# Products of a constant tile on TensorE, ahead of an attention and expert kernel's first maxima

## The chip, the cores and the metric

The kernel runs on one core of a Trainium2 chip. The time is the device time of one execution in microseconds, and a kernel's time is the median of its runs. The engines are TensorE (PE, with its loads of weights as PEld), VectorE (DVE), ScalarE (ACT), GpSimd (POOL) and SyncE (SP, which issues most of the transfers). Each has a queue of its own that it works in order.

## The reference

Attention for 4 batches of 8 heads, 576 tokens, 64 columns; its result, 2304 tokens of 512 columns, goes through a layer of 8 experts of which each token uses one.

```python
q_rot, k_rot = (rotate(q), rotate(k))
scores = scale * np.matmul(q_rot, k_rot.transpose(0, 1, 3, 2))
scores = scores - np.max(scores, axis=-1, keepdims=True)
attn = np.exp(scores)
attn = attn / (np.sum(attn, axis=-1, keepdims=True) + 1e-09)
attn_out = np.matmul(attn, v)
...
expert_idx = np.argmax(logits, axis=1)          # logits of x and the experts' embeddings
h = np.maximum(x[mask] @ w1[e], 0.0)
out[mask] = gate_w[mask, None] * (h @ w2[e])
```

## The kernel before

The attention works on 16 pairs of heads. A pair has nine steps: four tiles of 128 tokens for each of its two heads, and step 4, which holds the last 64 tokens of both. Work is put on a list with a due time in steps (`at(time, function, ...)`), pair `i` starting at time `9*i`; the list is sorted and emitted, and each engine works its part of it in that order.

For a pair, these functions matter:

- `rope` rotates q and k by products with cosines and sines (VectorE for pair 0 and for k of pair 1, GpSimd otherwise), casts the result to 16 bits on ScalarE (`qhi`, `khi`, line 133) and takes the rest (`qlo`, `klo`, line 138). `place` copies these by DMA to the operands of the scores (`QAB`, `KA`, `KB`).
- `maxmm` (line 171) multiplies q by k for one step: two products of 288 columns into a tile `mx` of two PSUM banks, columns 0 to 287 of each bank. `maxred` (line 175) takes the maximum of each row on VectorE. For pairs 0 to 2 the operands are `qhi` and `khi` themselves, with 64 rows, so that no copy is waited for. The maxima are only a shift against overflow.
- `maxend` turns a pair's nine maxima on TensorE (`mt`, line 182), casts them to a row on ScalarE and sends it by DMA into row 64 of `QB`.
- `smm` makes the scores of a step: four products of 288 columns (lines 196 and 199) into a tile `st`. `sexp` (line 209) takes the exponential on ScalarE, `ssub` (line 218) splits off the low half on VectorE.
- `ve` (line 112) multiplies v by the experts' embeddings, ten small 32-bit products. `pv` (lines 234 to 239) multiplies the exponentials by v, step by step, seven and a half steps behind the scores.

`mx` and `st` come from one pool `sps` of three tiles, tag `s`: a product into a new tile waits until the tile that stood in that place three tiles earlier was read.

The maxima of pair 0 are due from -21 to -17, those of pair 1 from -5 to 3, a step apart, so that the last four of pair 1 lie between the scores of pair 0; those of pair 2 from 4.5 on. The prologue (`first`, at -60) starts the loads. Behind the attention come the experts' products.

Of the kernel before, what the change touches and what calls it, by code (L numbers as in the profile page):

```python
# [6 lines left out]
F32 = mybir.dt.float32  # L7
F16 = mybir.dt.float16
# [30 lines left out]
def attention(tc, ctx0, ctx, ctx2, ins, xs, R, at, bank, cfg):  # L39
    nc = tc.nc  # L40
# [3 lines left out]
    const = ctx.enter_context(tc.tile_pool(name="aconst", bufs=1))  # L44
# [3 lines left out]
    sps = ctx.enter_context(tc.tile_pool(name="asps", bufs=3, space=PSUM))  # L48

    cost = rp.tile([128, S], F32, name="cost", bufs=1)  # L50
    sint = rp.tile([128, S], F32, name="sint", bufs=1)
    shiftt = const.tile([128, 1], F32, name="shiftt")
    nc.vector.memset(shiftt, SHIFT)
    NB = cfg.get("nb", 4)
# [85 lines left out]
    def place(i, nm, part):  # L140

        n, t = i % NB, st[i][nm + part]
        for h in range(2):
# [9 lines left out]
            else:  # L153
                nc.sync.dma_start(out=KB[n][0:64, c], in_=t[r])

    def maxmm(i, s):
        n = i % NB
        if s == 0:
            st[i]["m9"] = tp.tile([128, 9], F32, tag="m9", name=f"m9_{i}")
        ps = sps.tile([128, 2, 512], F32, tag="s", name=f"mx_{i}_{s}")  # L160
        st["mx", i, s] = ps
        hs = [(0, 64, 0), (64, 64, 1)] if s == 4 else [(0, 128, 0 if s < 4 else 1)]
        for r0, m, h in hs:
            for c in range(2):
                q, k = slice(s * 128 + r0, s * 128 + r0 + m), slice(h * S + c * 288, h * S + c * 288 + 288)
                lt, rt = QA[n][:, q], KA[n][:, k]
                if i < cfg.get("mdir", 1):

                    r = slice(64 * h, 64 * h + 64)
                    lt, rt = st[i]["qhi"][r, q.start - h * S:q.stop - h * S], st[i]["khi"][r, c * 288:c * 288 + 288]  # L170
                nc.tensor.matmul(ps[r0:r0 + m, c, :288], lhsT=lt, rhs=rt, start=True, stop=True)  # L171
# [86 lines left out]
    RL = cfg.get("rlead", 13)  # L258
    PVL = cfg.get("pvlead", 7)
    at(-60, first)  # L260
    for n in range(NB):
        at(-60 + .1 * n, nc.gpsimd.memset, KB[n][64:65, :], 1.0)
    start = cfg["start"]
# [5 lines left out]
    for i in range(NPAIR):  # L269
# [37 lines left out]
        for s in range(9):  # L307
            ev(f"S{s}", g0 + s, smm, i, s)
            ev(f"E{s}", g0 + s + .1, sexp, i, s)
            ev(f"U{s}", g0 + s + cfg.get("sst", 1.05), ssub, i, s)  # L310
            mev(f"M{s}", m0 + md * s + cfg.get("mmt", .2), maxmm, i, s)
            mev(f"C{s}", m0 + md * s + cfg.get("mct", .25), maxred, i, s)
            ev(f"P{s}", g0 + PVL + s + cfg.get("pvt", .3), pv, i, s)
            if s in (4, 8):
                ev(f"X{s // 5}", g0 + PVL + s + cfg.get("pe0", 1.04), pvend, i, s // 5, 0)
                ev(f"Y{s // 5}", g0 + PVL + s + cfg.get("pe1", 1.06), pvend, i, s // 5, 1)
# [403 lines left out]
class Schedule:  # L720
# [3 lines left out]
    def at(self, g, f, *a):  # L724
        self.T.append((g, len(self.T), f, a))
# [13 lines left out]
def build(tc, ins, out, cfg=None):  # L739
    cfg = {**TIMES, **(cfg or {})}  # L740
    nc = tc.nc
    with ExitStack() as ctx:
# [14 lines left out]
        mctx, actx2, actx, actx0 = [ctx.enter_context(ExitStack()) for _ in range(4)]  # L757
        if True:
            PVL = attention(tc, actx0, actx, actx2, ins, xs, R, sc.at, bank, cfg)
            for k in range(6):  # L760
                sc.at(cfg.get("setup", (-59.5, -25, -13, -12, -20, -8))[k], R.setup, k)
# [194 lines left out]
```

## Time and profile before

| | |
|---|---|
| median of 3 runs | 595.16 us (593.59 to 597.38) |
| the profiled execution | 591.15 us, of which the span from the first to the last instruction is 589.4 us |
| TensorE busy | 522.8 us, 89% of the span |
| VectorE busy | 522.4 us, 89% |
| ScalarE, GpSimd busy | 346.0 us (59%), 258.5 us (44%) |

Times in the rows count from the span's start. A row of the timeline has the start, the duration (of all instructions merged in it), engine, source line, operation, output and inputs, and how many; in brackets the idle time ahead of it and what ended it. The durations of products on TensorE are modelled and overlap; the distance from one start to the next tells how fast they run. The granted clock of TensorE is given as a share of its full speed.

### The profile page before, as it was taken

The numbers are of one execution on the slowest core, as the hardware profiler recorded it, in microseconds if no ns is written. First come the engines' busy times: TensorE is split into PE (matmuls) and PEld (weight loads), VectorE is DVE, ScalarE is ACT, GpSimd is POOL, SyncE is SP. The second block draws the span as 40 slices with busy tenths as digits, with TensorE's granted clock in tenths as the row PEclk, the third lists the DMA queues.
The fourth block names the chain that finished last, engine by engine and source line by source line (L and its number), as shares of the span: only waits on it lengthen the run. The fifth ranks groups of instructions, "written<-read, shape, count | busy, mean of one in ns | idle before, by whom it ended". The sixth has DMA issues, their size and how long they took to land. (4 is left out here: it accounts for less than half of the span.)

```text
span 589.4 us, 16094 instructions
## 1 busy us (share of the span) xinstructions
PE 522.8 (89%) x6222; PEld 403.3 (68%) x6222; DVE 522.4 (89%) x810; ACT 346.0 (59%) x578; POOL 258.5 (44%) x162
## 2 busy tenths in 40 slices
PE   1599898898898889788897989999999999999993
PEld 0336687776687777677686977767767767767761
DVE  5988889999999998999896665699999999999981
ACT  2143435464643546246356562588989989989962
POOL 5669847477657576621004231312422422423211
PEclk9999989899998989799898989999999999999998
DMA  8586566468565574423318410268986114431100
GB/s 279 149 246 193 140 172 167 137 172 213 146 179 152 173 202 133 131 73 88 106 47 288 127 29 20 91 206 298 317 302 208 39 57 157 127 137 38 56 20 31
DMA packets 42914, 86.13 MB, mean 146 GB/s; under 512 B 8390, under 2 KB 25670, under 8 KB 42832
## 3 DMA queue, kind: packets, MB, share of 16 engines
q1 hardware_dynamic: 39312, 74.46, 42.5%
q0 software_dynamic: 3520, 10.58, 5.6%
q8 instruction: 51, 0.84, 0.6%
q14 instruction: 31, 0.25, 0.1%
HBM read 115.84 MB, written 10.56 MB: 214 GB/s over the span
## 5 line engine op out<-in xcount | busy, mean ns | idle before, releaser
L652 DVE SCALAR_TENSOR_TENSOR w<-raw,w 128x1024 f16<-128x1024 f32 x148 | 177.0, 1236 | 9.4 <-ACT w L651 9.1
L209 ACT ACTIVATE p<-st 128x576 f32<-128x576 f32 x144 | 93.4, 649 | 136.2 <-PE st L199 134.7
L651 ACT ACTIVATE w<-raw 128x1024 f16<-128x1024 f32 x148 | 148.3, 1055 | 0.0
L688 PEld LDWEIGHTS <-w 128*128 128x128 f16 x2112 | 121.3, 99 | 4.7
L218 DVE TENSOR_TENSOR p<-p 128x576 f16<-128x576 f32 x112 | 124.4, 1115 | 0.0
L688 PE MATMUL h<-xTm,w 128*128 128x128 f16 x2112 | 123.6, 220 | 0.0
L709 PE MATMUL yp<-w,hT 128*128 128x512 f16 x528 | 120.8, 379 | 0.0
L175 DVE TENSOR_REDUCE m<-mx 128x1 f32<-128x576 f32 x144 | 105.1, 747 | 14.1 <-PE mx L171 13.7
L714 POOL DMA_INDIRECT out<-y,sidx x22 | 32.8, 1489 | 159.7 <-ACT y L713 159.7
L239 PE MATMUL pv<-V,p 128*128 128x73 f16 (+1 forms) x640 | 86.1, 202 | 1.7 <-DVE p L218 1.7
L709 PEld LDWEIGHTS <-hT 128*128 128x128 f16 x528 | 50.7, 98 | 53.0 <-issue 0.2
L237 PE MATMUL pv<-V,p 128*128 128x73 f16 (+1 forms) x640 | 86.4, 204 | 0.0
L238 PE MATMUL pv<-V,p 128*128 128x72 f16 (+1 forms) x640 | 86.0, 205 | 0.0
L237 PEld LDWEIGHTS <-p 128*128 128x128 bf16 (+1 forms) x640 | 74.1, 116 | 0.0
L196 PE MATMUL st<-QAB,KA 128*128 128x288 f16 (+1 forms) x320 | 65.1, 309 | 5.9 <-DVE m L175 5.2
L239 PEld LDWEIGHTS <-p 128*128 128x128 f16 (+1 forms) x640 | 67.5, 107 | 2.3 <-DVE p L218 2.3
L238 PEld LDWEIGHTS <-p 128*128 128x128 bf16 (+1 forms) x640 | 67.0, 106 | 0.0
L199 PE MATMUL st<-QAB,KB 65*128 65x288 f16 (+1 forms) x320 | 65.2, 308 | 0.0
L234 PE MATMUL pv<-V,p 128*128 128x73 f32 (+1 forms) x320 | 61.6, 277 | 0.0
L171 PE MATMUL mx<-KA,QAB 128*128 128x288 f16 (+1 forms) x260 | 51.0, 298 | 8.7 <-DVE m L175 5.7
L234 PEld LDWEIGHTS pv<-V,p 128*128 128x128 f32 (+1 forms) x320 | 50.0, 195 | 9.7 <-issue 5.6
L138 POOL TENSOR_TENSOR qlo<-q,qhi 128x576 f16<-128x576 f32 x14 | 20.5, 1465 | 64.4 <-ACT qhi L133 64.4
(157 smaller groups left out, 692.7 us busy)
## 6 DMA issues: line engine op xcount, KB each, us to landing
raw<-w SPq DMA_DIRECT2D x152, 512.0 KB
q<-qk SPq DMA_DIRECT2D x16, 576.0 KB
k<-qk SPq DMA_DIRECT2D x16, 576.0 KB
vt<-vt SPq DMA_DIRECT2D x16, 320.0 KB
v<-v SPq DMA_DIRECT2D x16, 320.0 KB
QAB<-qhi SPq DMA_DIRECT2D x32, 144.0 KB
KA<-khi SPq DMA_DIRECT2D x64, 72.0 KB
xs<-x SPq DMA_DIRECT2D x8, 512.0 KB
```

The costliest lines, as they stand in the source:

```text
L175: nc.vector.tensor_reduce(out=st[i]["m9"][:, s:s + 1], in_=st.pop(("mx", i, s))[:, :, :288], op=ALU.max, axis=AX.XY)
L199: nc.tensor.matmul(ps[r0:r0 + m, c, :288], lhsT=KB[n][0:65, col], rhs=QB[n][0:65, h * S + c * 288:h * S + c * 288 + 288], start=False, sto ...
L209: nc.scalar.activation(out=p.rearrange("p (c x) -> p c x", c=2), in_=st.pop(("s", i, s))[:, :, :288], func=AF.Exp, scale=0.125)
L218: nc.vector.tensor_tensor(out=lo, in0=p, in1=hi, op=ALU.subtract)
L234: nc.tensor.matmul(o[:, 0:73], lhsT=P[ksl][0][:, qc:qc + m], rhs=V32[i % NV][:, h, kk], start=(kk == 0), stop=False, skip_group_check=True)
L237: nc.tensor.matmul(o[:, 0:73], lhsT=ph, rhs=vv[:, 0:73], start=(kk == 0), stop=False, skip_group_check=True)
L238: nc.tensor.matmul(o[:, 1:73], lhsT=ph, rhs=vv[:, 73:145], start=False, stop=False, skip_group_check=True)
L239: nc.tensor.matmul(o[:, 0:73], lhsT=pl, rhs=vv[:, 0:73], start=False, stop=(kk == 4), skip_group_check=True)
L651: nc.scalar.activation(out=d[:, 0], in_=raw[c], func=AF.Copy, scale=SW)
L652: nc.vector.scalar_tensor_tensor(out=d[:, 1], in0=raw[c], scalar=SW, in1=d[:, 0], op0=ALU.mult, op1=ALU.subtract)
L688: nc.tensor.matmul(ps[:, f], lhsT=wd[:, wi, jj * 512 + f * 128:jj * 512 + f * 128 + 128], rhs=xt[:, xi, 2 * jp + jj], start=(jp == 0 and k ...
L709: nc.tensor.matmul(ps, lhsT=ht[:, hi, 2 * c + ii], rhs=wd[:, wi, ii * 512:(ii + 1) * 512], start=(c == 0 and k == 0), stop=(c == 3 and k = ...
```

## The change

A tile `wz` of 128 x 512 ones, 16 bits, is written by VectorE as its first instruction. In the prologue TensorE makes 30 products of `wz` by itself, 512 columns wide, into a tile `warm` of the pool `sps`. In pairs 0 and 1, ahead of the two products of each step but step 4, it makes two products of 224 columns into columns 288 to 511 of that step's own tile `mx`, which nobody reads.

```diff
+    wz = const.tile([128, 512], F16, name="wz")
+    nc.vector.memset(wz, 1.0)
...
+    def warm(n):
+        ps = sps.tile([128, 2, 512], F32, tag="s", name="warm")
+        for _ in range(n):
+            nc.tensor.matmul(ps[:, 0], lhsT=wz[:, 0:128], rhs=wz, start=True, stop=True)
+
     def maxmm(i, s):
...
         st["mx", i, s] = ps
+        if i < 2 and s != 4:
+            for c in range(2):
+                nc.tensor.matmul(ps[:, c, 288:512], lhsT=wz[:, 0:128], rhs=wz[:, 0:224], start=True, stop=True)
         hs = [(0, 64, 0), (64, 64, 1)] if s == 4 else [(0, 128, 0 if s < 4 else 1)]
...
     at(-60, first)
+    at(-58.95, warm, 30)
```

TensorE's queue at the end of pair 0's maxima, before. `mx_8` is the last step's tile, `khi`, `qhi` the rotated operands, `ve` and `mt` as above, and the last `mx_0` is pair 1's:

```order
L171 MATMUL mx_8_263<-khi_200,qhi_181 128x288 [waits DVE_49]
L171 LDWEIGHTS qhi_181
L171 MATMUL mx_8_263<-khi_200,qhi_181 128x288
L112 MATMUL ve_267<-enB,vt_176 128x2x8 [waits DMAHW1_49]
L112 MATMUL ve_267<-enB,vt_176 128x2x8 x4
L182 MATMUL mt_286<-ident,m_0_216 9x128 [waits DVE_49]
L171 LDWEIGHTS qhi_273 [waits PE_49,Activation_49]
L171 MATMUL mx_0_306<-khi_280,qhi_273 128x288 [waits Activation_49]
```

The same place now (lines of the changed file):

```order
L172 LDWEIGHTS wz
L172 MATMUL mx_8_310<-wz 128x224 [waits DVE_49]
L172 MATMUL mx_8_310<-wz 128x224
L182 LDWEIGHTS qhi_214
L182 MATMUL mx_8_310<-khi_233,qhi_214 128x288
L115 MATMUL ve_316<-enB,vt_209 128x2x8 [waits DMAHW1_49]
L115 MATMUL ve_316<-enB,vt_209 128x2x8 x4
L193 MATMUL mt_335<-ident,m_0_249 9x128 [waits DVE_49]
L172 MATMUL mx_0_355<-wz 128x224 [waits PE_49]
L172 MATMUL mx_0_355<-wz 128x224
L182 LDWEIGHTS qhi_322 [waits Activation_49]
L182 MATMUL mx_0_355<-khi_329,qhi_322 128x288 [waits Activation_49]
```

The wait for VectorE, which frees the tile, now stands at the first product of `wz`; the wait for ScalarE's `khi` stays at the real product, so the products of `wz` for pair 1's step 0 stand ahead of it.

TensorE's queue between the first score tile `st_0` and the second, before:

```order
L199 LDWEIGHTS KB_131
L199 MATMUL st_0_340<-QAB_129,KB_131 128x288
L171 LDWEIGHTS qhi_273
L171 MATMUL mx_5_347<-khi_280,qhi_273 128x288 [waits DVE_49]
L171 MATMUL mx_5_347<-khi_280,qhi_273 128x288
L196 LDWEIGHTS KA_130
L196 MATMUL st_1_352<-QAB_129,KA_130 128x288 [waits DVE_49]
```

And now:

```order
L210 LDWEIGHTS KB_133
L210 MATMUL st_0_397<-QAB_131,KB_133 128x288
L172 LDWEIGHTS wz
L172 MATMUL mx_5_404<-wz 128x224 [waits DVE_49]
L172 MATMUL mx_5_404<-wz 128x224
L182 LDWEIGHTS qhi_322
L182 MATMUL mx_5_404<-khi_329,qhi_322 128x288
L207 LDWEIGHTS KA_132
L207 MATMUL st_1_411<-QAB_131,KA_132 128x288 [waits DVE_49]
```

Two products and two loads of weights are new between the score tiles; nothing else has changed places.

## Rows read from the trace of the kernel before

**Rows 1.** The page, busy time (share of the span) and instructions of each engine.

```profile
PE 522.8 (89%) x6222; PEld 403.3 (68%) x6222; DVE 522.4 (89%) x810; ACT 346.0 (59%) x578; POOL 258.5 (44%) x162
```

**Rows 2.** Busy time by stage: length, then PE, PEld, DVE, ACT, POOL, clock, DMA, GB/s.

```profile
13.00:30.00 17.00, 10.39 (x43) 5.87 (x42) 15.38 (x24) 2.46 (x7) 12.15 (x9) 1.00 0.59 154
30.00:46.00 16.00, 14.22 (x57) 5.23 (x56) 13.71 (x15) 7.37 (x13) 11.46 (x8) 1.00 0.85 235
46.00:62.00 16.00, 15.81 (x115) 10.92 (x115) 12.06 (x14) 4.89 (x11) 12.11 (x8) 1.00 0.62 173
62.00:76.00 14.00, 11.87 (x156) 9.60 (x154) 13.86 (x22) 5.90 (x11) 11.59 (x7) 0.99 0.64 174
76.00:79.00 3.00, 3.00 (x29) 2.54 (x28) 3.00 (x6) 1.28 (x4) 0.00 (x0) 0.50 0.51 136
```

**Rows 3.** TensorE's timeline, a maxima's step and the next.

```profile
32.00 0.66 PE L171 MATMUL mx<-khi,qhi 64*128 64x288 f16 x2
...
33.67 0.66 PE L171 MATMUL mx<-khi,qhi 64*128 64x288 f16 x2
```

**Rows 4.** TensorE's timeline, two score steps with value products, and 62 us.

```profile
53.08 0.68 PE L196 MATMUL st<-QAB,KA 128*128 128x288 f16 x2
...
56.00 0.68 PE L196 MATMUL st<-QAB,KA 128*128 128x288 f16 x2
...
62.07 0.24 PE L237 MATMUL pv<-V,p 128*64 128x73 f16 x1
```

**Rows 5.** TensorE's timeline, score steps and `ve` after 62 us.

```profile
65.42 0.41 PE L196 MATMUL st<-QAB,KA 128*128 128x288 f16 x2
...
66.15 0.34 PE L234 MATMUL pv<-V,p 128*128 128x73 f32 x2
...
71.19 0.41 PE L196 MATMUL st<-QAB,KA 128*128 128x288 f16 x2
...
73.28 1.29 PE L112 MATMUL ve<-enB,vt 128*128 128x16 f32 x10 [0.99 <-DVE xe L255]
```

**Rows 6.** TensorE's timeline, from pair 0's last maxima to the first scores.

```profile
23.40 1.30 PE L171 MATMUL mx<-khi,qhi 64*128 64x288 f16 x4 [0.46 <-DVE m L175]
24.63 2.31 PE L112 MATMUL ve<-enB,vt 128*128 128x16 f32 x10
...
27.90 3.07 PE L171 MATMUL mx<-khi,qhi 64*128 64x288 f16 x12 [0.74 <-ACT khi L133]
30.95 0.64 PE L196 MATMUL st<-QAB,KA 128*128 128x288 f16 x2
```

**Rows 7.** VectorE's waits, 26 to 62 us: total us, times, longest.

```profile
DVE m L175 <- PE mx L171: 6.2, 6, 2.2
DVE V L118 <- ACT V L117: 1.3, 1, 1.3
```

**Rows 8.** ScalarE's timeline, behind `ve`.

```profile
26.98 0.27 ACT L116 ACTIVATE V<-ve 128x80 f16<-128x80 f32 x1 [10.17 <-PE ve L112]
...
27.18 0.67 ACT L133 CAST khi<-k 128x576 f16<-128x576 f32 x1
```

**Rows 9.** The first product on TensorE, the first maximum on VectorE.

```profile
13.17 1.60 PE L171 MATMUL mx<-khi,qhi 64*128 64x288 f16 x6 [13.17 <-ACT khi L133]
...
16.98 0.74 DVE L175 TENSOR_REDUCE m<-mx 128x1 f32<-128x576 f32 x1
```

**Rows 10.** VectorE's timeline, its first wait.

```profile
5.45 0.76 DVE L126 TENSOR_TENSOR q<-q,cost 128x576 f32<-128x576 f32 x1 [3.64 <-DMA q<-qk]
```

**Rows 11.** VectorE's timeline, pair 1's last four maxima.

```profile
32.70 0.76 DVE L175 TENSOR_REDUCE m<-mx 128x1 f32<-128x576 f32 x1 [0.47 <-PE mx L171]
34.36 0.76 DVE L175 TENSOR_REDUCE m<-mx 128x1 f32<-128x576 f32 x1 [0.91 <-PE mx L171]
36.03 0.76 DVE L175 TENSOR_REDUCE m<-mx 128x1 f32<-128x576 f32 x1 [0.91 <-PE mx L171]
...
39.75 0.74 DVE L175 TENSOR_REDUCE m<-mx 128x1 f32<-128x576 f32 x1
```

## Prediction, made before the result was known

> **What bounds the kernel now.** I read the page's busy times first. TensorE and VectorE are both busy for 89% of the span [rows 1], which does not say what the first 80 us are worth, and the change lies there alone. The table of stages [rows 2] is the next view. In 30 to 46 us TensorE is busy 14.22 of 16 us and VectorE 13.71; in 46 to 62 us TensorE is busy 15.81 and VectorE only 12.06; in 62 to 76 us it is the other way round (11.87 against 13.86 of 14). So TensorE limits up to 62 us and VectorE limits after that.
>
> The reason is TensorE's clock. The granted clock in [rows 2] reads 1.00 up to 76 us and 0.50 in 76 to 79 us, but before 62 us I trust the spacing of the products instead: the first change that it shows is the fall at 76 us, so the 1.00 ahead of it may be no record at all. Between 32.00 and 33.67 us six products of 288 columns start one behind the other, 0.278 us each [rows 3]; between 65.42 and 66.15 us six products of the same width take 0.73 us, 0.122 us each [rows 5]. That is the lower of the two levels (1.2 GHz) before, the upper (2.4 GHz) after; the change is at 62.07 us, where products of 73 columns shorten from 0.26 us [rows 4]. The price of it: one score step with its share of the value products lasts 2.92 us (53.08 to 56.00 us) [rows 4] and later 1.92 us (65.42 to 71.19 us, three steps) [rows 5].
>
> What can be won is bounded by VectorE's waits. From 26 to 62 us it waits 6.2 us in six pieces for the maxima's products and 1.3 us behind `ve` [rows 7], together 7.5 us. Everything else of that time it works already.
>
> **The burst in the prologue.** The constant tile is written by VectorE before all else; VectorE then waits 3.64 us for the first load [rows 10], so this costs nothing. The thirty products of 512 columns have no row in the trace; their price scales from [rows 3, 5] by columns: 0.278 x 512/288 = 0.49 us each at the lower level, 0.22 us at the upper, so 14.8 or 6.5 us in all. They start at about 1 us, when `wz` is there, and end between 8 and 16 us. The first real product starts at 13.17 us, and its maximum is taken at 16.98 us [rows 9]; even 16 us plus one group and one pair of real products (0.43 + 0.56 us) comes to 17 us. I cost the burst at nothing: VectorE's own work on the rotations covers it, and were that cover gone it would be up to 3 us. The burst takes one of the three score buffers, but only TensorE uses it before the next product in that buffer.
>
> **The groups ahead of the maxima.** Eight of nine steps in pairs 0 and 1 get two products of 224 columns each. A group costs 2 x 0.278 x 224/288 = 0.43 us at the lower level and 2 x 0.122 x 224/288 = 0.19 us at the upper. The ends are 0 (it fits into an idle time) and 0.56 us (it costs as much as two products of 288 columns). I take 0.43, by columns, as the loads of weights run beside the products. Each group waits for the same buffer as the real product behind it, so it can't use the time in which the buffer is still read; it stands between the release and the product.
>
> - Pair 0, steps 0 to 3: covered by VectorE, which between the first maximum and the others still has rotations in its queue. Steps 5 to 8: 4 x 0.43 = 1.73 us in a run of TensorE that had 0.46 us of idle time left [rows 6], so `ve` starts 1.27 us later. Behind `ve` are ScalarE's copies and, in their queue, the cast of pair 1's `khi` [rows 8], for which TensorE waits at 27.90 us [rows 6]. So **1.27 us** pass on.
> - Pair 1, step 0: free, it fits into the 0.74 us in which TensorE waits for `khi`. Steps 1 to 3: the run from 27.90 us on goes over into the first score tile at 30.95 us without idle time [rows 6]: 3 x 0.43 = **1.30 us**.
> - Pair 1, steps 5 to 8: TensorE has no idle time here and VectorE waits for it [rows 7, 11]. 4 x 0.43 = 1.73 us, of which the last 0.43 is hidden: VectorE takes that maximum only at 39.75 us, because its queue is full from 36.03 us on [rows 11]. **1.30 us**.
>
> The sum is 3.87 us if the clock stays at the lower level in this stretch. It passes on: from 36 us VectorE, from 46 us TensorE works almost without a gap [rows 2], and both queues are in order.
>
> **Does the clock stay low?** This decides the sign. The burst itself is dense, and I expect it to lift the clock while it runs. What comes after it is not: in 13 to 30 us TensorE is busy 10.39 of 17 us by ends that are modelled, with waits for VectorE and ScalarE [rows 2, 6], and the groups add 16 products of 0.2 us there. In 62 to 76 us TensorE was busy 11.87 of 14 us and the clock still fell to 0.50 [rows 2]. So the clock should be down again when the part begins that TensorE limits. And a TensorE that is nearly always busy was not enough to lift it: it did 14.22 of 16 us in 30 to 46 us, with no change of spacing until 62 us. In that stretch the groups replace little idle time; they mainly lengthen it.
>
> The Trainium skill, TensorE: Matmul & The Clock Gate, section Why this matters for your kernels, has it that keeping TensorE busy without a break brings the clock to full. The trace disagrees for this mix of products, by the 14.22 of 16 us just named. By that rule the sum would be that of the first rival below. The same page's section HAM oscillation speaks against the change: a burst followed by waits loses the clock again. The fall after 62 to 76 us agrees.
>
> **The rivals.**
> 1. The clock stays up from the burst on. For it: the groups add dense products where the trace shows thin ones. Against it: the fall at 76 us after a busier stretch. It gives back what TensorE's slowness costs: three steps at 2.92 instead of 1.92 us (3.0 us), the waits before the maxima in 30 to 36 us (0.47 + 0.91 + 0.91 = 2.29 us, part of the 6.2), `ve` at 1.29 instead of 2.31 us (1.0 us) [rows 4, 5, 6, 11], less three groups at 0.19 us: -5.7 us, 589.5 us.
> 2. The clock rises only for pair 1's run and falls in the stretch that VectorE limits. It then wins 2.29 us and pays about 0.6 us for groups: -1.7 us. With the clock up for half that run it comes to about 0. 593.5 to 596 us.
> 3. Slower by over 1%: the rise at 62 us [rows 4] comes later. It came 16 us into the stretch that TensorE limits; nothing ties it to a given step, and with all work shifted by 3.9 us it may meet a step some places further on. Each further step at the lower level costs 2.92 - 1.92 = 1.0 us. With three it is 3.9 + 3.0 = 6.9 us, 602.1 us; the point is 2.1 further steps.
>
> That the products are dropped because nothing reads them is no case: the built program has 62 products and 62 loads of weights more in TensorE's queue.
>
> **How the numbers follow.** The profiled execution took 591.15 us, 4.0 below the median of 595.16 of the three runs. On its own time the sum gives 595.0, on the median 595.16 + 3.87 = **599.0 us**. About 1% (6 us) is what a measurement of this kernel tells from no change. Chances: forecast 0.62, rival 1 0.13, rival 2 0.18, rival 3 0.07. Runs of this kernel lie 3.8 us apart, so of the forecast 0.05 falls above 601.1, and of rival 1 about half below 589.2. Faster by over 1%: 0.07; slower by over 1%: 0.11; within: 0.82. The range goes from 590 (most of rival 2, half of rival 1) to 602 (price of a group up to 0.56 us: 7 groups more by 0.13 is 0.9 us, and the spread of the runs).
>
> **What would show it.** Right: thirty products that get faster part of the way; then spacing of 0.27 us for 288 columns at 32 us; the first score tile near 33.5 us instead of 30.95; pair 1's maxima step of 2.1 us instead of 1.67; a rise of the clock near 62 to 66 us. Wrong: a spacing of 0.12 us before 50 us, or VectorE's 6.2 us of waits for the maxima gone.

## The result, and the profile after

The changed kernel takes 598.2 us (median of 20 runs, 593.07 to 602.02), the kernel before 594.56 us in the same session (20 runs, 587.12 to 597.66). By the medians it is 3.6 us slower; the ratio is 1.009, 95% interval [1.0061, 1.0118]. Forecast were 599.0 us, within 1% of before. A ratio here is made without those runs of a kernel that lie over 1.5% above its own fastest, which takes 7 of 20 runs from the kernel before and 1 of 20 from the changed one and so lifts the ratio; the medians are of all runs, and by them it is 1.006.

The profiled execution of the changed kernel took 599.48 us, span 597.6 us, 8.2 us more than the span before. Its busy times answer to [rows 1]: TensorE has 24 us more, VectorE 3 us less.

```profile
PE 546.8 (91%) x6284; PEld 415.0 (69%) x6284; DVE 519.2 (87%) x811; ACT 345.3 (58%) x578; POOL 256.5 (43%) x162
```

The table of stages, with the columns of [rows 2]; the stretch ahead of 13 us and the burst in it are new.

```profile
0.00:13.00 13.00, 9.15 (x32) 3.72 (x33) 7.42 (x22) 3.17 (x5) 6.99 (x11) 1.00 0.87 280
13.00:30.00 17.00, 14.20 (x59) 5.83 (x58) 14.21 (x24) 2.43 (x7) 10.95 (x8) 0.50 0.65 158
30.00:46.00 16.00, 15.27 (x64) 6.00 (x63) 11.55 (x13) 6.17 (x11) 10.52 (x8) 0.50 0.90 233
46.00:62.00 16.00, 14.88 (x97) 9.88 (x97) 12.94 (x14) 4.88 (x11) 11.74 (x7) 0.50 0.63 174
62.00:76.00 14.00, 12.81 (x147) 9.53 (x145) 12.33 (x20) 6.65 (x12) 11.14 (x7) 0.80 0.51 133
```

The clock column now has a record from the burst on: full from 6.2 us, 0.50 from 13.0 us, full again at 67.6 us. With 0.50 on record, products of 288 columns stand as far apart as before (0.45 us for two at 32.52 us, 0.46 us at 32.59 us before). So the 1.00 that the profile before shows ahead of its first change is no record, and the spacing of the products was the right thing to read. From 13 to 62 us TensorE is busy 44.35 of 49 us and stays at the lower level, 1.2 GHz.

TensorE's timeline: the burst; the first groups and products of pair 1; the scores of pair 0's steps 0 to 2; pair 1's score steps 0, 1 and 5. They answer to [rows 3 to 6].

```profile
1.46 8.96 PE L162 MATMUL warm<-wz 128*128 128x512 f16 x30 [1.46 <-DVE wz L54]
...
28.09 0.63 PE L182 MATMUL mx<-khi,qhi 64*128 64x288 f16 x2 [0.37 <-ACT khi L136]
28.66 0.56 PE L172 MATMUL mx<-wz 128*128 128x224 f16 x2
29.14 0.66 PE L182 MATMUL mx<-khi,qhi 64*128 64x288 f16 x2
29.73 0.56 PE L172 MATMUL mx<-wz 128*128 128x224 f16 x2
...
32.52 0.66 PE L207 MATMUL st<-QAB,KA 128*128 128x288 f16 x2
32.97 0.69 PE L210 MATMUL st<-QAB,KB 65*128 65x288 f16 x2
33.45 0.58 PE L172 MATMUL mx<-wz 128*128 128x224 f16 x2
33.97 0.66 PE L182 MATMUL mx<-khi,qhi 64*128 64x288 f16 x2
34.55 0.66 PE L207 MATMUL st<-QAB,KA 128*128 128x288 f16 x2
...
36.59 0.66 PE L207 MATMUL st<-QAB,KA 128*128 128x288 f16 x2
...
55.92 0.68 PE L207 MATMUL st<-QAB,KA 128*128 128x288 f16 x2
...
58.84 0.68 PE L207 MATMUL st<-QAB,KA 128*128 128x288 f16 x2
...
69.39 0.41 PE L207 MATMUL st<-QAB,KA 128*128 128x288 f16 x2
```

The burst ends at 10.4 us and hides behind VectorE's rotations; 12 of its products start in the 4.7 us up to the rise of the clock, 18 in the 4.2 us behind it. A group stands 0.48 to 0.50 us ahead of its product in pair 1's first steps and 0.52 us between the scores. The score steps of pair 0 are 2.04 us apart; before, 32.00 to 33.67 us was one such step, 1.67 us [rows 3]. The first score comes 1.57 us later than in [rows 6], pair 1's second step at 58.84 instead of 56.00 us [rows 4], 2.84 us later, and its sixth at 69.39 instead of 65.42 us [rows 5], 3.97 us later, because the clock rose 5.4 us later.

VectorE's waits from 26 to 62 us, which answer to [rows 7]: 8.7 us instead of 7.5.

```profile
DVE m L186 <- PE mx L182: 6.9, 7, 1.3
DVE V L121 <- ACT V L120: 1.8, 1, 1.8
```

The first score's 1.57 us is less than the sum of the two terms that lie ahead of it, 1.27 and 1.30 us. The reason is an addition of pair 1's rotation on VectorE, at 18.4 us in both. After:

```profile
17.62 0.74 DVE L131 TENSOR_TENSOR k<-k,sint 128x576 f32<-128x576 f32 x1
18.39 0.76 DVE L133 TENSOR_TENSOR k<-k 128x576 f32<-128x576 f32 x1
...
18.98 1.42 POOL L129 TENSOR_TENSOR q<-q,cost 128x576 f32<-128x576 f32 x1 [2.91 <-DMA KA<-khi]
```

Before:

```profile
17.77 1.87 POOL L126 TENSOR_TENSOR q<-q,cost 128x576 f32<-128x576 f32 x1 [1.67 <-DMA KA<-khi]
...
18.42 1.84 DVE L130 TENSOR_TENSOR k<-k 128x576 f32<-128x576 f32 x1
```

The same addition takes 0.76 us where GpSimd starts its product behind it, and 1.84 us where GpSimd's was already running: 1.08 us that this execution happened to save. When GpSimd starts differs between executions of one kernel: here it waited for a DMA (`KA<-khi`), in the two other executions of the changed kernel it started at 16.31 and 16.45 us. In every other kernel below whose position is used, the addition took 1.84 or 1.85 us. The Trainium skill, SBUF — State Buffer, section SBUF: two separate sides, has these two engines share a port that one of them holds for a whole instruction; the two rows agree. To compare executions I therefore count from the first maximum on VectorE (16.98 us before, 16.95 after) and take off what the last product and the addition of pair 1's rotation behind it took longer than in the profile before. With that the first score is 15.57 - (13.97 - 1.08) = 2.68 us later.

### The profile page after: what moved, and what is told of

Its sections match the earlier page's. It is cut to its first block, busy times and chain, and to the rows that moved or that the text cites. A ratio compares the mean times of both kernels' runs of the same rounds, so it can differ in the third digit from the quotient of the medians.

```text
span 597.6 us, 16218 instructions
## 1 busy us (share of the span) xinstructions
PE 546.8 (91%) x6284; PEld 415.0 (69%) x6284; DVE 519.2 (87%) x811; ACT 345.3 (58%) x578; POOL 256.5 (43%) x162
## 5 line engine op out<-in xcount | busy, mean ns | idle before, releaser
L229 DVE TENSOR_TENSOR p<-p 128x576 f16<-128x576 f32 x112 | 120.5, 1081 | 0.0
L250 PE MATMUL pv<-V,p 128*128 128x73 f16 (+1 forms) x640 | 88.3, 205 | 1.6 <-DVE p L229 1.6
L248 PE MATMUL pv<-V,p 128*128 128x73 f16 (+1 forms) x640 | 88.6, 207 | 0.0
L249 PE MATMUL pv<-V,p 128*128 128x72 f16 (+1 forms) x640 | 88.2, 208 | 0.0
L248 PEld LDWEIGHTS <-p 128*128 128x128 bf16 (+1 forms) x640 | 75.6, 119 | 0.0
L207 PE MATMUL st<-QAB,KA 128*128 128x288 f16 (+1 forms) x320 | 67.3, 317 | 4.1 <-DVE m L186 3.7
L250 PEld LDWEIGHTS <-p 128*128 128x128 f16 (+1 forms) x640 | 68.8, 109 | 2.3 <-DVE p L229 2.3
L249 PEld LDWEIGHTS <-p 128*128 128x128 bf16 (+1 forms) x640 | 68.3, 108 | 0.0
L210 PE MATMUL st<-QAB,KB 65*128 65x288 f16 (+1 forms) x320 | 67.2, 316 | 0.0
L245 PE MATMUL pv<-V,p 128*128 128x73 f32 (+1 forms) x320 | 63.2, 283 | 0.0
L245 PEld LDWEIGHTS pv<-V,p 128*128 128x128 f32 (+1 forms) x320 | 52.0, 202 | 10.0 <-issue 5.5
L182 PE MATMUL mx<-KA,QAB 128*128 128x288 f16 (+1 forms) x260 | 52.4, 304 | 7.0 <-DVE m L186 3.9
```

The costliest lines, as they stand in the source:

```text
L207: nc.tensor.matmul(ps[r0:r0 + m, c, :288], lhsT=KA[n][:, col], rhs=QA[n][:, h * S + c * 288:h * S + c * 288 + 288], start=True, stop=False)
L229: nc.vector.tensor_tensor(out=lo, in0=p, in1=hi, op=ALU.subtract)
L245: nc.tensor.matmul(o[:, 0:73], lhsT=P[ksl][0][:, qc:qc + m], rhs=V32[i % NV][:, h, kk], start=(kk == 0), stop=False, skip_group_check=True)
L248: nc.tensor.matmul(o[:, 0:73], lhsT=ph, rhs=vv[:, 0:73], start=(kk == 0), stop=False, skip_group_check=True)
L249: nc.tensor.matmul(o[:, 1:73], lhsT=ph, rhs=vv[:, 73:145], start=False, stop=False, skip_group_check=True)
L250: nc.tensor.matmul(o[:, 0:73], lhsT=pl, rhs=vv[:, 0:73], start=False, stop=(kk == 4), skip_group_check=True)
```

## The experiments

**The burst alone** (twice), **the groups alone** (twice), and the changed kernel itself twice more. The burst alone is

```diff
-        if i < 2 and s != 4:
-            for c in range(2):
-                nc.tensor.matmul(ps[:, c, 288:512], lhsT=wz[:, 0:128], rhs=wz[:, 0:224], start=True, stop=True)
```

and the groups alone

```diff
-    at(-58.95, warm, 30)
```

> The thirty products of the prologue alone, without the groups ahead of the maxima. Theory (the groups cost, the burst costs nothing and its clock is lost again): the clock rises near 6 us and is down again by 13 to 17 us; the first score product starts at 30.9 to 31.2 us as before (32.5 with the whole change), pair 1's second score step at 56.0 us (58.8 with the change), and the median is that of before within 1.5 us. Rival A (the burst helps on its own): first scores before 30.5 us. Rival B (the burst is what costs): first scores near 32.5 us and a median 3 us above before.

> The burst alone, a second time, beside the kernel before and the next three on one chip. Theory (the burst costs nothing): ratio to the kernel before 0.997 to 1.003, score steps 1.66 us apart, low clock from about 15 to 63 us. Rival (the burst costs some 2.4 us after 80 us, by more time at the lower clock): ratio 1.003 to 1.007, like the first time (1.0051).

> The groups ahead of the maxima alone, without the burst. Theory: everything that the whole change does to the time: first score product at 32.4 to 32.7 us, 2.04 us from one score step to the next in the first four instead of 1.67, pair 1's second score step at 58.6 to 59 us, median 3 to 4 us above before. Rival (burst and groups only work, or only cost, together): first scores near 31 us, median as before.

> The groups alone, a second time. Theory (three terms of 1.31, 1.37 and 1.24 us that pass on to the end): 3.9 us, ratio 1.005 to 1.009. Rival (they cost some 7 us, as the first time's 1.013 has it, by something after 70 us): ratio above 1.010.

> The whole change once more, for a second profile. Theory: the burst and the clock as in the first profile; counted from the first maximum on VectorE, pair 1's second score step 3.7 to 4.1 us later than before when VectorE's rotation of k ahead of the second maximum takes 1.84 us as before, 2.8 when it takes 0.76 us as in the first profile. Rival (the 2.8 us are what the change costs): 2.8 with either.

> The changed kernel itself, beside its two parts. Theory (only the groups cost): ratio 1.005 to 1.009, within 0.003 of the groups alone. Rival (burst and groups both cost): above the groups alone by 0.004 or more.

| kernel | median us (runs) | before | ratio, 95% interval | rise behind 60 us | score step | first score, corrected | first score to pair 1's second step |
|---|---|---|---|---|---|---|---|
| before | | | | 62.2 | 1.66 | 13.97 | 25.05 |
| burst | 594.36 (12) | 591.91 (23) | 1.0051 [1.0009, 1.0093] | 63.1 | 1.66 | 13.97 | 25.09 |
| burst, again | 596.07 (12) | 594.88 (29) | 1.0052 [1.0008, 1.0095] | 62.9 | 1.66 | 13.96 | 25.17 |
| groups | 598.79 (6) | 591.91 (23) | 1.013 [1.0066, 1.0193] | 66.5 | 2.04 | 16.66 | 26.27 |
| groups, again | 598.15 (6) | 594.88 (29) | 1.0106 [1.0036, 1.0175] | 69.0 | 2.04 | 16.65 | 26.26 |
| changed, one run | 592.79 (1) | | | 74.6 | 2.04 | 16.65 | 26.29 |
| changed, again | 596.80 (12) | 594.88 (29) | 1.0107 [1.0062, 1.0152] | 73.9 | 2.04 | 16.65 | 26.27 |

The column of the rise is the time at which the clock rises behind 60 us; "corrected" counts from the first maximum as said above. The last two columns agree to 0.1 us from one execution to the next: the groups bring the first score 2.68 us later and pair 1's second step another 1.2 us, with the burst or without it. The burst brings neither. In both executions with the burst alone the clock rose 4.9 and 5.1 us after the span's start, was down again at 15.2 and 15.3 us, and rose where it rises without the burst.

The times fit less well than the positions. Expected were, for the burst, a median within 1.5 us of before and then a ratio of 0.997 to 1.003; for the groups 3 to 4 us and then 1.005 to 1.009, which the changed kernel should have shown too. Measured were 2.5 us and 1.0052, 6.9 us and 1.0106, and 1.0107, all above; the second runs of burst and groups fell into the ranges of their rivals.

Whether the groups' delay reaches the end is read from all the runs. Each has a mean granted clock; over the 68 runs of the kernel before that stand beside the experiments, the time falls by 3.2 us per 0.01 of it (correlation -0.89). The straight line through them gives 594.4 us at 0.955, the mean clock of the 12 runs with the groups alone; these took 598.4 us on average, 4.0 us more. (Neither kernel has a record of the clock ahead of its first rise, so the two means compare; the groups' rise comes 4.3 and 6.8 us later, and what that costs lies within the 4.0 us. A mean with the burst in it also counts the low stretch from 13 us on.)

The burst's cost is not settled. Its medians lie 2.5 and 1.2 us above those of before, and both intervals just leave out 1; yet, counted from the first maximum, nothing in the first 62 us is later, and in the one session that has both, the changed kernel's ratio (1.0107) is that of the groups alone (1.0106). An estimate from the runs: with the 47.8 us at the lower level that both profiles of the burst have on record up to the rise taken out of each mean clock, the 24 runs lie 0.3 us below the straight line, with a standard error of 0.3 us. So behind the rise the burst costs nothing that the clock there does not account for; that clock was lower (0.953 against 0.959 on average), and whether the burst brings this about is open. If it costs anything, it does so behind 62 us.

**Pair 0's groups and pair 1's groups apart**, each with the burst:

```diff
-        if i < 2 and s != 4:
+        if i == 0 and s != 4:
```

(and `i == 1`).

> Burst, and the groups ahead of pair 0's maxima alone. Theory (the prediction's first term): the four groups of steps 5 to 8 pass on 1.27 us by way of `ve` and the cast of pair 1's `khi`; counted from the first maximum on VectorE (16.98 us before), the first product of pair 1 comes 1.1 to 1.4 us later than the 10.9 us of before, unless GpSimd's rotations lie so that VectorE's own rotation of k is 1.1 us shorter, as in the profile of the whole change. The four score steps stay 1.67 us apart. Rival (VectorE's queue hides pair 0's groups altogether): no shift.

> Burst, and the groups ahead of pair 1's maxima alone. Theory (the second and third terms): from pair 1's first product to the first score product 4.3 to 4.5 us instead of 3.05, then four score steps 2.04 us apart instead of 1.67; pair 1's second score step 2.4 to 2.9 us later than before, counted from the first maximum. Rival (only groups in both pairs cost): no shift.

TensorE's timeline with pair 0's groups only, where the first maximum came at 17.69 us:

```profile
26.65 2.31 PE L115 MATMUL ve<-enB,vt 128*128 128x16 f32 x10
28.80 0.37 PE L193 MATMUL mt<-ident,m 128*9 128x128 f32 x1
29.92 3.07 PE L182 MATMUL mx<-khi,qhi 64*128 64x288 f16 x12 [0.74 <-ACT khi L136]
32.97 0.64 PE L207 MATMUL st<-QAB,KA 128*128 128x288 f16 x2
```

With pair 1's groups only, first maximum at 17.26 us:

```profile
24.91 2.31 PE L115 MATMUL ve<-enB,vt 128*128 128x16 f32 x10
...
28.18 0.64 PE L182 MATMUL mx<-khi,qhi 64*128 64x288 f16 x2 [0.37 <-ACT khi L136]
...
32.60 0.66 PE L207 MATMUL st<-QAB,KA 128*128 128x288 f16 x2
...
34.64 0.66 PE L207 MATMUL st<-QAB,KA 128*128 128x288 f16 x2
```

Pair 0's groups move pair 1's first maximum product from 10.92 to 12.23 us behind the first maximum, 1.31 us, and nothing after it: 3.05 us to the first score as before [rows 6], and 25.12 us from there to pair 1's second step. Pair 1's groups leave that product at 10.92 us, with 0.37 instead of 0.74 us of waiting for `khi` (step 0's group lies in it), and bring the first score 4.42 us behind it, 1.37 us more. The terms act apart and add: 1.31 + 1.37 = 2.68. From the first score to pair 1's second step this kernel took 26.83 us, half a microsecond more than the changed kernel; TensorE waited there for a maximum (0.39 us at 47.76 us). Counted from the first maximum that step is 3.15 us later than before, more than the 2.4 to 2.9 us expected. The two kernels' times, 601.59 and 597.71 us, are single runs and decide nothing.

**Four products per group**, with the burst:

```diff
-            for c in range(2):
-                nc.tensor.matmul(ps[:, c, 288:512], lhsT=wz[:, 0:128], rhs=wz[:, 0:224], start=True, stop=True)
+            for c in range(4):
+                nc.tensor.matmul(ps[:, c % 2, 288:512], lhsT=wz[:, 0:128], rhs=wz[:, 0:224], start=True, stop=True)
```

> Burst, and four instead of two products of 224 columns in each group. Theory (each group is paid at the lower clock, about 0.37 to 0.43 us for two products): the first four score steps 2.4 to 2.5 us apart, pair 1's second score step at 61.5 to 62.5 us, median 6 to 8 us above before. Rival (it is a matter of dose: denser work lifts the clock): products of 288 columns 0.12 us apart before 45 us, and a median below that of the change.

601.08 us (6 runs), ratio 1.0148 [1.0084, 1.0212]. The score steps are 2.41 us apart, again 0.37 us more. Counted as above, pair 1's second step is 8.0 us later than before, against 3.9 with groups of two. The median, 9.2 us above before, and pair 1's second step, at 64.53 us, are more than was expected. The clock falls at 14.8 us and rises at 72.9 us: with twice the products in TensorE's queue ahead of each step it rises no sooner. That speaks against the first rival in the form that the change has.

**TensorE's waits filled.** If it is the waits between the burst and 48 us that lose the clock, filling them should keep it up. This kernel has no groups in pairs 0 and 1; it puts full products of 512 columns into a PSUM tile of their own (so that they wait for no score tile), as many as fit each wait, and puts groups ahead of pair 2's maxima from the fourth step on. Its edit, against the changed kernel:

```diff
-        if i < 2 and s != 4:
+        if i == 2 and s >= 3:
...
+    def fill(k, n, new=False):
+        if new:
+            st["fill", k] = bank("fill", k)
+        for _ in range(n):
+            nc.tensor.matmul(st["fill", k], lhsT=wz[:, 0:128], rhs=wz, start=True, stop=True)
+
-    at(-58.95, warm, 30)
+    at(-58.95, fill, 1, 36, True)
+    at(-19.75, fill, 1, 15)
+    at(-19.15, fill, 1, 9)
...
+    for s, n in zip(range(5, 9), (8, 13, 10, 8)):
+        at(s - .4, fill, 1, n)
```

A second version trims it where products lay on the path (one instead of two behind pair 0's last maxima, four instead of six behind `ve`; 13 instead of 9 in the wait at 17 us; 10, 11, 8, 6 at the end). A third is the second without the 36 of the prologue.

> No groups ahead of the maxima of pairs 0 and 1; instead 36 products of 512 columns in the prologue and 89 more, each put where TensorE waits for another engine up to 48 us, and groups of two ahead of pair 2's maxima from step 3 on. Theory (TensorE's clock is what 28 to 62 us wait for, and it stays up only if the waits are filled): products of 288 columns 0.12 us apart from 13 us on, first score product near 30.2 us, VectorE's waits for the maxima's products between 26 and 62 us down from 6.2 us to under 3, pair 1's second score step 2 to 4 us earlier than the 56.0 of before, median 2 to 5 us below before. Rival (VectorE sets the pace whatever TensorE's clock): the clock up but pair 1's second score step within 1 us of 56.0. Rival (the filling is not enough): 0.27 us apart at 32 us, and a median above before.

> The filling of before's waits (the run with 36 products in the prologue and 89 more), cut where that run shows it to be on the path: one instead of two products behind each of pair 0's last maxima, four instead of six ahead of pair 0's turned maxima, 10, 11, 8 and 6 instead of 8, 13, 10 and 8 ahead of score steps 5 to 8; 13 instead of 9 where TensorE still waited 1.25 us. Theory (the clock is worth time, the filling costs what it adds on the path): the clock stays up past 60 us, first score product 1 us earlier than the 32.45 of that run, pair 1's second score step near 53.5 us instead of 55.4 there and 56.0 before, and a median 4 to 8 us below before. Rival (the trimmed filling lets the clock fall before 50 us): products of 288 columns 0.27 us apart again, pair 1's second score step at 56 us or later, median within 2 us of before.

> The trimmed filling without its burst: no product before the first real one, then the same filling in TensorE's waits from 17 us on. Theory (only filling at the time when TensorE limits matters): the clock is low at first, the filling lifts it between 17 and 30 us, the score steps are 1.1 to 1.2 us apart, ratio 0.992 to 0.997. Rival (without a burst the clock doesn't rise, and the filling only lengthens TensorE's path): first rise after 60 us, score steps 2.0 us apart or more, ratio above 1.003.

| kernel | median us (runs) | before | ratio, 95% interval | clock up, in us |
|---|---|---|---|---|
| filled | 589.63 (12) | 591.91 (23) | 0.9926 [0.9873, 0.998] | 6.0 to 210.8 |
| trimmed | 588.38 (12) | 592.64 (16) | 0.994 [0.9904, 0.9976] | 4.6 to 25.0, 28.4 to 209.4 |
| trimmed, no burst | 592.23 (12) | 594.88 (29) | 0.9984 [0.9938, 1.0031] | 15.4 to 53.0, 63.2 to 213.4 |

Stages of the trimmed version:

```profile
13.00:30.00 17.00, 16.09 (x75) 6.33 (x74) 14.83 (x24) 2.46 (x6) 12.77 (x10) 0.90 0.56 155
30.00:46.00 16.00, 15.52 (x89) 6.71 (x89) 15.01 (x16) 6.86 (x12) 11.47 (x7) 1.00 0.92 245
46.00:62.00 16.00, 15.88 (x194) 11.66 (x194) 14.41 (x20) 6.75 (x14) 15.19 (x10) 1.00 0.56 167
62.00:76.00 14.00, 11.61 (x164) 9.52 (x163) 13.93 (x21) 7.05 (x14) 7.82 (x6) 1.00 0.75 205
```

The score steps of the trimmed version are 1.16 us apart, and VectorE's waits for the maxima are down from 6.2 us [rows 7] to

```profile
DVE m L181 <- PE mx L177: 3.8, 7, 1.3
```

Here the first rival's world is real but for 25.0 to 28.4 us, and the kernel is faster than before: 4.3 us by medians, where the rival's sum said 5.7. The filling itself lies on TensorE's path in places: pair 1's maxima and their filling stand one behind the other, 0.67 us per step. Counted as above, the first score comes 1.07 us later than before, pair 1's second step 1.12 us and its sixth 3.17 us earlier; so a good part of the gain arises behind the second step, where the kernel before was still at the lower level.

The first filled version met its expected median (2.3 us below before), but not the positions: the first score came at 32.45 instead of near 30.2 us, VectorE's waits for the maxima were 5.0 us instead of under 3, and pair 1's second step came at 55.41 us, within the 1 us of 56.0 that its first rival had named. Counted as above, that step is 1.35 us earlier than before, its sixth 3.40 us. That rival, VectorE setting the pace whatever the clock, still does not fit: the score steps of 1.16 us and the sixth step's gain are there.

Without the burst the filling lifts the clock all the same, at 15.4 us, 3.8 us after TensorE's first product. TensorE's stages up to the fall and behind it, and the row ahead of the fall:

```profile
15.40:30.00 14.60, 14.48 (x76) 5.83 (x73) 13.16 (x21) 2.46 (x6) 10.87 (x8) 1.00 0.50 128
30.00:53.00 23.00, 21.55 (x154) 11.31 (x153) 19.41 (x20) 9.04 (x17) 17.57 (x11) 1.00 0.81 212
53.00:63.20 10.20, 10.20 (x80) 6.48 (x78) 5.66 (x7) 3.23 (x7) 6.42 (x5) 0.50 0.47 155
```

```profile
52.51 0.40 PE L205 MATMUL st<-QAB,KB 65*128 65x288 f16 x2 [1.45 <-DMA QAB<-mr]
```

TensorE had run so far ahead that it met the transfer of pair 1's maxima and waited 1.45 us; at 53.0 us the clock was down, and the next score step, with its group, was 3.28 us long (54.89 to 58.17 us). So the burst is not needed to lift the clock, and the mechanism half of that run's theory held; its time did not (forecast 0.992 to 0.997). Whether the burst itself or only this fall makes the difference to the trimmed version is open, as the intervals overlap.

## Why the prediction was right

- **Who limits, and at which clock.** Right. The lower level up to 62 us, which I took from the spacing, is now on record: 0.50 in all of 13 to 62 us.
- **The burst.** Right on the trace: 1.46 to 10.4 us, products getting faster part of the way, nothing later behind it. The sum's zero has a reserve of up to 2.5 us by the medians, which goes with a lower clock behind 62 us and whose cause is open.
- **The price of a group**, 0.43 us by columns, ends 0 and 0.56. In the score steps it is 0.37 us (2.04 - 1.67): a group stands 0.52 us ahead of its product, but 0.48 us behind the start of the scores' second half (32.97 to 33.45 us), where the product itself stood 0.62 us behind it before. In pair 0, 1.31 us of delay and 0.46 us of idle time used [rows 6] make 0.44 us each; in pair 1's first steps 1.37/3 = 0.46 us. Scaling by columns was good to 0.06 us. (The range allows for 7 groups at 0.56 us; the sum charges ten, which would be 1.3 us more instead of 0.9.)
- **The three terms**: 1.27, 1.30 and 1.30 us were forecast; 1.31, 1.37 and 1.24 us (26.29 - 25.05) were measured, 3.92 against 3.87 us. The chain through `ve`, ScalarE's copies and the cast of `khi` for the first term is shown by the run with pair 0's groups alone: the idle time ahead of pair 1's product is still 0.74 us, ended by `khi`.
- **Passes on to the end.** Right in size: 4.0 us at equal clock for the groups alone, 3.6 us by the medians of 20 runs. That the forecast was met to 0.8 us is in part luck: the second comparison of the changed kernel gave 1.9 us by medians, its three profiled executions span 591.0 to 597.6 us, and the later rise (below) cost time that the sum did not have and the clock behind it partly gave back.
- **The first score near 33.5 us.** 32.52 us in the profile shown, 34.37 and 33.70 us in two more. The scatter is VectorE's rotations against GpSimd's, which the sum did not have.
- **The clock does not stay up.** Right, and so the sign. The rule that I quoted from the Trainium skill, TensorE: Matmul & The Clock Gate, section Why this matters for your kernels (a TensorE kept busy without a break comes to full clock), fails for this mix as the prediction had it: 15.27 of 16 us busy in 30 to 46 us and the clock at 0.50. That stretch, like the one with the prediction's 14.22 of 16 us, has breaks; plainer is 53.0 to 63.2 us of the trimmed version without a burst, 10.20 of 10.20 us busy by modelled ends and the clock at 0.50 throughout. With full products in the waits, 15.52 of 16 us in 30 to 46 us, the clock stays at 1.00. So TensorE's busy time alone doesn't tell the two cases apart. The mix of products is the likelier reason, as a low clock rose at 15.4 us in the version without a burst, behind the first six maxima products and in the middle of fifteen full ones; but no run changes the mix alone, and in the stretch at 1.00 the clock was already up when it began. Rival 2, a clock that is up for pair 1's maxima only, was seen in no run.
- **The rise near 62 to 66 us, and rival 3.** Wrong in part. The rise came at 67.6 us in the profile shown, at 73.9 and 74.6 us in two more, one score step later than before in the first and three in the others, so the condition of rival 3 was met, in two of three executions in full. Its price was wrong for the whole: I charged 1.0 us for each further step at the lower level. Up to pair 1's sixth step most of that is there (6.4 and 6.5 us later than before, counted from the first maximum, in the two executions with three steps, where the terms alone make 3.9), but the kernel gets part of it back. Where the clock rose at 67.6 us it fell again at 77.8, 94.9 and 112.0 us. Where it rose at 73.9 us it stayed up for 75 us (the clock is the third column from the end):

```profile
62.00:74.00 12.00, 12.00 (x107) 8.88 (x107) 9.22 (x13) 3.16 (x5) 8.56 (x5) 0.51 0.42 100
74.00:149.00 75.00, 67.00 (x934) 55.74 (x931) 73.14 (x120) 38.63 (x82) 50.80 (x31) 1.00 0.64 179
```

That execution's span is 594.0 us, 3.6 us below the other's. I did not reckon with falls behind 80 us that differ from one execution to the next.

The profiled spans differ by 8.2 us, twice the sum. Up to pair 1's sixth step it is 3.97 us, 1.1 of it behind the second step, where the clock rose later. Behind 69 us the changed kernel's profile has 61.1 us at the lower level, that of before 44.5; 16.6 us by 0.27 us (the 3.2 us per 0.01 above, and 0.01 of 590 us of span is 11.8 us at half speed) is an estimate of 4.5 us. So by this estimate half of the difference of the two profiles is scatter, and only the runs could give the size.

## What to carry to other kernels

Products whose only purpose is the clock must stand in TensorE's waits and wait for nothing that the real ones wait for; put behind the same buffer and ahead of the real product they were pure length, 0.37 to 0.46 us each group here. A burst at the start gained nothing by itself here; with the waits up to the stretch that TensorE limits filled, the kernel became 0.6 to 0.7% faster. Price an edit in the stage where it lies, from positions counted from a common event, and take its effect on the whole from runs compared at equal granted clock.

## What was not expected of the hardware

- A clock held up to the stretch behind 62 us stayed up for long without any filling there: in the trimmed version from 62 to 209 us TensorE was busy 127.08 of 147 us and the clock read 1.00 throughout, while before it fell at 75.8 us behind a stretch with 11.47 of 13.6 us busy. All three filled versions first fell between 209 and 214 us after that. The changed kernel's clock, which rose at 73.9 and 74.6 us, also stayed up for 75 us in both executions. What ties the later falls to the earlier course was not tried.
- A VectorE product or addition of 128 x 576 32-bit values takes 0.74 to 0.76 us alone and 1.28 to 1.95 us where one of GpSimd was already running, and GpSimd's first product for pair 1 starts anywhere from 15.89 to 18.98 us in these profiles: 0.5 to 1.1 us of scatter in the first 20 us, as large as a term of the sum.
